# Two attention-time weight blocks: the join on VectorE cut in halves and the five steps after the load spread over half-steps

## The chip, the cores and the metric

The kernel runs on one core of one Trainium2 chip. The metric is the device time of one execution in microseconds (us); the kernel before took 747.65 us (median of 3 runs, 746.45 to 749.12). A core has five engines that each work through their own instructions in order: TensorE (PE, with its weight loads PEld), VectorE (DVE), ScalarE (ACT), GpSimd (POOL) and SyncE (SP, which issues most DMAs).

## The reference

Attention with a learned relative-position bias, for 4 batches of 8 heads, 576 positions, 64 channels, and then a feed-forward layer over all 2304 tokens:

```
scores = q @ k.T / sqrt(64) + bias          # bias: a small MLP of log-distances, 8 heads
attn   = exp(scores - max);  attn /= attn.sum() + 1e-9
x      = (attn @ v)  as [2304, 512]
h = x @ w_in                                 # 512 x 2048
g = h if h >= 1, 0 if h <= -1, else (h + 1)**2 / 4
out = g @ w_out                              # 2048 x 512
```

The feed-forward weights arrive as 64-bit integers' bytes (each element 8 bytes in memory) and are turned into 32-bit floats on the chip. Each float operand of a matmul is split into a high part (type fp32r) and a low remainder, and the products high x high, high x low, low x high are summed.

## The kernel before, in words

The program has three stages. First the bias is made (lines 217 to 350). Then the attention runs over 16 units `n` (line 624): a unit is two heads of one batch, with 5 row groups `k` each (128 rows for `k` 0 to 3, the last 64 rows of both heads together for `k` = 4). Last comes the feed-forward part over blocks of tokens.

In one attention unit, for every row group and both heads `j`: PE makes scores into a PSUM tile `S` (lines 455 and 456, two tiles in turn, so the next but one score waits until DVE has read this one); DVE adds the bias, writes `e` to SBUF and takes the row's extremum (line 458; line 478 for the tile `S_L` of `k` = 4); ACT takes the exponential (line 465); PE transposes `e` into PSUM tiles `T` (line 521; four in turn, shared with `O` and `R`). A transposed tile is split into `hi` and `lo`. For some tiles ACT casts `hi` (line 496) and DVE subtracts for `lo` (line 497). For `T_0_1`, `T_2_0`, `T_2_1`, `T_3_0` and `T_3_1` ACT copies the tile to SBUF as `c` (line 501), `hi` is cast by POOL (line 503, `T_0_1` and `T_3_0`) or by DVE (line 505, the other three), and POOL subtracts for `lo` (line 506). Then PE multiplies with the values (lines 559 and 561): `O_0` for the first half of the rows (`hi_0`, `lo_0`), `O_1` for the second half (`hi_1`, `lo_1`); within each, the five `hi` products stand ahead of the five `lo` products. After `O_1`, PE transposes the row sums into `R` (line 545), which closes a unit. Unit n's `O_1` and `R` stand on PE among the scores of unit n + 1: what the trace shows between two `R` is one unit's work, shifted. POOL also makes the low parts of keys (`ls`, line 136, two instructions) and values (`vs`, line 136), and issues the load `qa` (line 167); DVE casts `kh` (line 163) and `vs` (line 178).

Which instruction stands where on an engine is decided when the program is built: a scheduler orders them by its own cost estimates, except those marked with `keep` or `pool`, which stay in the order in which the code issues them (on their engine). So an edit at one place can move unmarked neighbours on every engine.

Into the attention's half-steps (`step`, line 621: `10 * n + i_`, ten to a unit) the kernel plans other work by the table `WQ`: four weight blocks, `(f, o)` = (0,0), (0,1), (1,0), (1,1), are loaded at half-steps 49, 59, 89, 99 and made from half-steps 53, 63, 93, 103 on, so in units 5, 6, 9 and 10. The making has five steps (`weight_ahead`, line 94): `shift` and `sign` on ACT (lines 105 and 112), `join` on DVE (line 116: an or of the shifted digits and the sign, 128x512, in place in the tile `a`), `high` on DVE (line 121: a cast of `a` to `w0h` or `w1h`) and `rest` on POOL (line 125: the remainder `w0l` or `w1l`). The other 28 blocks are made with the same function during the feed-forward part. The tiles `raw` and `a` are single buffers: the next load into them waits for their last reader.

Of the kernel before, what the change touches and what calls it, by code (L numbers as in the profile page):

```python
# [10 lines left out]
I32 = mybir.dt.int32  # L11
U16 = mybir.dt.uint16
AF = mybir.ActivationFunctionType
ALU = mybir.AluOpType
# [6 lines left out]
NT, DM, DFF = B * S, H * D, 2048  # L21
# [26 lines left out]
def attn_cpb_moe_kernel(ctx, tc, qk, vL, cb, win, wout, lw, ident, ii, out):  # L48
    nc = tc.nc
# [38 lines left out]
    def ring(o, i):  # L88
        return [rpool[i % 3].tile([P, DM], F32R, tag=f"w{o}{x}", name=f"w{o}{x}{i}") for x in "hl"]
# [4 lines left out]
    def weight_ahead(f, o, rp):  # L94

        w = {}
        src = wout[f * P : f * P + P] if o else win[f]

        def load():
            w["raw"] = rp.tile([P, DM, 2], I32, tag="raw", name=f"raw{f}{o}")  # L100
            nc.sync.dma_start(out=w["raw"].rearrange("p a b -> p (a b)"), in_=src.bitcast(I32))

        def shift():
            raw = w["raw"]
            keep(nc.scalar.activation(raw[:, :, 0], raw.bitcast(U16).rearrange("p a (b c) -> p a b c", c=2)[:, :, 0, 1], AF.Identity, scale=2.0**-13, bias=floor_s))

        def sign():
            if f < 2:
                w["a"] = rp.tile([P, DM], F32, tag="a", name=f"a{f}{o}")
            else:  # L110
                w["a"] = full[o, f]
            keep(nc.scalar.activation(w["a"], w["raw"][:, :, 1].bitcast(F32), AF.Prelu, scale=2.0**-112, alpha=-(2.0**32)))

        def join():
            t = w["a"].bitcast(I32)
            keep(nc.vector.scalar_tensor_tensor(out=t, in0=t, scalar=3, in1=w["raw"][:, :, 0], op0=ALU.logical_shift_left, op1=ALU.bitwise_or))

        def high():
            if f > 1:
                parts[o, f] = ring(o, f)  # L120
            keep(nc.vector.tensor_copy(parts[o, f][0], w["a"]))

        def rest():
            h, l = parts[o, f]
            keep(nc.gpsimd.tensor_tensor(out=l, in0=w["a"], in1=h.bitcast(F32), op=ALU.subtract))

        return load, shift, sign, join, high, rest

    qkv, bias = {}, {}
# [8 lines left out]
    def keep(ins):  # L138
        tc.keep_in_program_order(ins)
# [277 lines left out]
    with ExitStack() as ph:  # L417
# [173 lines left out]
        def plan(T, f):  # L591
            jobs.setdefault(T, []).append(f)
# [13 lines left out]
        for fo, (T, T1) in WQ.items():  # L606
            load, *fs = weight_ahead(*fo, rps[0])
            plan(T, load)
            for i, f in zip((0, 0, 1, 1, 2), fs):
                plan(T1 + i, f)  # L610

        def store_x(all_=False):
# [86 lines left out]
    with ExitStack() as ph:  # L699
# [197 lines left out]
        for f in range(2, NF):  # L897
            for o in range(2):
                m = 2 * f - 4 + 3 * o
                jobs[m] = weight_ahead(f, o, rps[m % 3 > 0])  # L900
# [12 lines left out]
        for k in range(2):  # L913
            t = T1 + 1 + 12 * k
# [17 lines left out]
        for blk in (0, TB):  # L932
            for m in range(2 * NF):
                f, j = m // 2, m % 2
# [4 lines left out]
                c = gp.tile([P, TH], F32, tag="c", name=f"c{blk}_{m}")  # L939
# [47 lines left out]
        for g in range(NG2):  # L987
            blk, f = b2, 2 * g
            for s_ in range(NS):
                t = NS * g + s_  # L990
# [110 lines left out]
```

## Time and profile before

| | us |
|---|---|
| median of the runs | 747.65 |
| profiled execution | 747.49 |
| its span, first to last instruction | 745.7 |
| units 5, 6, 9, 10, from `R` to `R` | 17.59, 17.35, 17.59, 17.31 |
| unit 3, which has neither a weight block nor another planned job | 15.96 |

The profiled execution is 1.8 us longer than its span, and 0.16 us under the median. In the rows below, times are us from the start of the span unless marked ns; a row of a timeline gives start, duration, engine, line, operation, output and inputs by name, shape, count, and in brackets how long the engine sat idle before it and what ended that.

### The profile page before, as it was taken

The numbers are of one execution on the slowest core, as the hardware profiler recorded it, in microseconds if no ns is written. First come the engines' busy times: TensorE is split into PE (matmuls) and PEld (weight loads), VectorE is DVE, ScalarE is ACT, GpSimd is POOL, SyncE is SP. The second block draws the span as 40 slices with busy tenths as digits, with TensorE's granted clock in tenths as the row PEclk, the third lists the DMA queues.
The fourth block names the chain that finished last, engine by engine and source line by source line (L and its number), as shares of the span: only waits on it lengthen the run. The fifth ranks groups of instructions, "written<-read, shape, count | busy, mean of one in ns | idle before, by whom it ended". The sixth has DMA issues, their size and how long they took to land. (4 is left out here: it accounts for less than half of the span.)

```text
span 745.7 us, 13716 instructions
## 1 busy us (share of the span) xinstructions
PE 701.6 (94%) x4640; PEld 620.3 (83%) x4640; DVE 541.5 (73%) x1047; ACT 516.4 (69%) x1151; POOL 519.2 (70%) x440
## 2 busy tenths in 40 slices
PE   5687999999999999999999999999999998999997
PEld 2234899998988889889988898898989987888896
DVE  7899888888898898886876866354465557666653
ACT  8896989888888889877565656444534446666563
POOL 8986777888878888852667677466655645666652
PEclk9999999999999999999999999999999999999999
DMA  8887799977997898634355554133021002000002
GB/s 231 239 268 227 200 250 244 305 204 183 263 234 196 201 256 205 156 113 147 113 177 162 189 155 138 43 96 75 1 65 32 1 4 82 1 1 1 0 1 85
DMA packets 58518, 103.37 MB, mean 139 GB/s; under 512 B 12480, under 2 KB 32464, under 8 KB 58448
## 3 DMA queue, kind: packets, MB, share of 16 engines
q1 hardware_dynamic: 56000, 92.44, 43.7%
q0 software_dynamic: 2304, 9.96, 6.4%
q8 instruction: 37, 0.61, 0.4%
q14 instruction: 33, 0.27, 0.1%
q10 hardware_dynamic: 144, 0.09, 0.1%
HBM read 67.38 MB, written 25.12 MB: 124 GB/s over the span
## 5 line engine op out<-in xcount | busy, mean ns | idle before, releaser
L951 POOL TENSOR_TENSOR gl<-c,gh 128x384 fp32r<-128x384 f32 x64 | 70.9, 1107 | 104.2 <-issue 86.8
L506 POOL TENSOR_TENSOR lo<-c,hi 128x512 fp32r<-128x512 f32 x75 | 101.5, 1369 | 29.7 <-DVE hi L505 27.1
L716 PE MATMUL y<-w1h,gl 128*128 128x512 f32 x288 | 114.0, 396 | 0.0
L716 PE MATMUL y<-w1l,gh 128*128 128x512 f32 x288 | 113.7, 395 | 0.0
L716 PE MATMUL y<-w1h,gh 128*128 128x512 f32 x288 | 112.0, 389 | 0.0
L465 ACT ACTIVATE e<-e,mx 128x576 f32<-128x576 f32 x128 | 100.6, 790 | 12.7 <-DVE mx L458 12.6
L458 DVE CUSTOM_DVE_ANT_0 e<-S,bias 128x576 f32<-128x576 f32 x128 | 94.3, 750 | 12.6 <-PE S L456 12.0
L455 PE MATMUL S<-kh,qa 128*128 128x288 f32 x256 | 78.4, 323 | 6.8 <-DVE mx L458 4.6
L769 ACT ACTIVATE c<-c,half_s 128x384 f32<-128x384 f32 x64 | 39.4, 616 | 60.7 <-DVE c L766 60.7
L456 PE MATMUL S<-ls,qa 128*128 128x288 f32 x256 | 72.3, 300 | 0.0
L521 PE MATMUL T<-id_s,e 128*128 128x128 f32 x512 | 70.7, 274 | 1.3 <-DVE lo L497 0.8
L977 POOL TENSOR_TENSOR gl<-c,gh 128x384 fp32r<-128x384 f32 x32 | 32.8, 1024 | 50.0 <-issue 23.3
L716 PEld LDWEIGHTS y<-w1h,gl 128*128 128x128 f32 x288 | 54.0, 187 | 11.6
L521 PEld LDWEIGHTS T<-id_s,e 128*128 128x128 f32 x512 | 58.7, 142 | 4.1 <-DVE lo L497 1.3
L284 ACT ACTIVATE u<-lw,nthr 128x576 f16<-128x576 f32 (+17 forms) x104 | 57.7, 644 | 5.1 <-PE B L303 2.7
L716 PEld LDWEIGHTS y<-w1l,gh 128*128 128x128 f32 x288 | 54.0, 187 | 8.0
L716 PEld LDWEIGHTS y<-w1h,gh 128*128 128x128 f32 x288 | 54.1, 188 | 7.7
L303 PEld LDWEIGHTS <-qh 128*32 128x32 f16 x704 | 19.1, 102 | 49.2 <-issue 21.2
L455 PEld LDWEIGHTS S<-kh,qa 128*128 128x128 f32 x256 | 48.2, 188 | 11.7 <-DVE mx L458 8.7
L772 DVE TENSOR_TENSOR c<-h,c 128x384 f32<-128x384 f32 x64 | 35.5, 554 | 26.8 <-ACT c L769 26.0
L286 POOL TENSOR_SCALAR u<-lw,thr 128x576 f16<-128x576 f32 (+17 forms) x36 | 51.5, 1442 | 4.3 <-PE B L303 3.1
L947 ACT CAST gh<-c 128x384 fp32r<-128x384 f32 x64 | 32.9, 513 | 30.7 <-DVE c L772 28.7
(264 smaller groups left out, 2117.5 us busy)
## 6 DMA issues: line engine op xcount, KB each, us to landing
bias_d<-y SPq DMA_DIRECT2D x36, 295.5 KB
qk<-in_qk_dram SPq DMA_DIRECT2D x16, 608.0 KB
qa<-in_qk_dram POOLq DMA_DIRECT2D x16, 608.0 KB, 7.0
x<-xT SPq DMA_DIRECT2D x48, 192.0 KB
raw<-in_win_dram SPq DMA_DIRECT2D x16, 512.0 KB
raw<-in_wout_dram SPq DMA_DIRECT2D x16, 512.0 KB
v<-in_vL_dram SPq DMA_DIRECT2D x16, 320.0 KB
qa<-ls SPq DMA_DIRECT2D x32, 152.0 KB
```

The lines of the kernel that those rows point to most:

```text
L284: tc.keep_in_program_order(nc.scalar.activation(u[:, :n_], lw1[:, :n_], AF.Sigmoid, bias=nthr[:, m : m + 1], scale=STEEP))
L286: EN[x].tensor_scalar(out=u[:, :n_], in0=lw1[:, :n_], scalar1=thr[:, m : m + 1], scalar2=None, op0=ALU.is_gt)
L455: nc.tensor.matmul(ps[:, hf, :HS], qs[:, qc], kh[:, kc : kc + HS], start=True, stop=False)
L456: nc.tensor.matmul(ps[:, hf, :HS], q0[:, qc], kl[:, kc : kc + HS], start=False, stop=True)
L458: nc.vector.tensor_tensor_reduce(out=ev.rearrange("p (a b) -> p a b", a=2), in0=ps[:, :, :HS], in1=bias[k][:, S * j : S * j + S].rearrange ...
L465: lambda ev=ev, j=j: nc.scalar.activation(ev, ev, AF.Exp, bias=mx[:, j : j + 1], scale=-1.0, accum_out=sm[:, 4 * j + k : 4 * j + k + 1])
L506: r = nc.gpsimd.tensor_tensor(out=lo, in0=m, in1=hi.bitcast(F32), op=ALU.subtract)
L521: nc.tensor.transpose(ps[:, tb, :], e[:, c0 : c0 + P], id_s)
L716: a = nc.tensor.matmul(out, w, x, start=start, stop=stop)
L769: keep(nc.scalar.activation(c, c, AF.Square, scale=0.5, bias=half_s))
L772: keep(nc.vector.tensor_tensor(out=c, in0=h, in1=c, op=ALU.max))
L951: keep(nc.gpsimd.tensor_tensor(out=gl, in0=c, in1=gh.bitcast(F32), op=ALU.subtract))
```

## The change

`join` takes a range of columns. For the first two `f` (the four blocks made in the attention) the function returns `first_half` and `second_half` in its place, so there are six steps after the load, and they are planned at half-steps T1 + 0, 0, 1, 2, 3, 4 (shift, sign, first half, second half, high, rest), where it was T1 + 0, 0, 1, 1, 2 (shift, sign, join, high, rest).

```diff
-        def join():
-            t = w["a"].bitcast(I32)
-            keep(nc.vector.scalar_tensor_tensor(out=t, in0=t, scalar=3, in1=w["raw"][:, :, 0], op0=ALU.logical_shift_left, op1=ALU.bitwise_or))
+        def join(c=slice(0, DM)):
+            t = w["a"].bitcast(I32)[:, c]
+            keep(nc.vector.scalar_tensor_tensor(out=t, in0=t, scalar=3, in1=w["raw"][:, c, 0], op0=ALU.logical_shift_left, op1=ALU.bitwise_or))
+
+        def first_half():
+            join(slice(0, DM // 2))
+
+        def second_half():
+            join(slice(DM // 2, DM))
...
+        if f < 2:
+            return load, shift, sign, first_half, second_half, high, rest
         return load, shift, sign, join, high, rest
...
             load, *fs = weight_ahead(*fo, rps[0])
             plan(T, load)
-            for i, f in zip((0, 0, 1, 1, 2), fs):
+            for i, f in zip((0, 0, 1, 2, 3, 4), fs):
                 plan(T1 + i, f)
```

What this does to the order on the engines is shown for unit 5 on two of them. In these rows the number behind a name is a buffer's, `lo_1` and `hi_1` are the parts of the second half of the rows, and `c` is ACT's copy of a transposed tile. Lines of the kernel after are 8 higher from line 134 on, and 6 higher for the cast and the remainder.

POOL before, from the remainder of the weight block on:

```order
L125 TENSOR_TENSOR w0l_120<-a_2863,w0h_119 128x512
L506 TENSOR_TENSOR lo_1_2921<-c_2927,hi_1_2920 128x4x128
L506 TENSOR_TENSOR lo_1_2921<-c_2936,hi_1_2920 128x4x128
L136 TENSOR_TENSOR vs_2954<-v_2769,vs_2954 128x10x64
L167 DMA qa_112<-in_qk_dram 64x2x1216
L503 CAST hi_1_2920<-c_3011 128x4x128
L506 TENSOR_TENSOR lo_1_2921<-c_3011,hi_1_2920 128x4x128
L506 TENSOR_TENSOR lo_1_2921<-c_3020,hi_1_2920 128x4x128
```

and now:

```order
L514 TENSOR_TENSOR lo_1_2921<-c_2927,hi_1_2920 128x4x128
L514 TENSOR_TENSOR lo_1_2921<-c_2936,hi_1_2920 128x4x128
L131 TENSOR_TENSOR w0l_120<-a_2863,w0h_119 128x512
L144 TENSOR_TENSOR vs_2955<-v_2769,vs_2955 128x10x64
L175 DMA qa_112<-in_qk_dram 64x2x1216
L511 CAST hi_1_2920<-c_3012 128x4x128
L514 TENSOR_TENSOR lo_1_2921<-c_3012,hi_1_2920 128x4x128
L514 TENSOR_TENSOR lo_1_2921<-c_3021,hi_1_2920 128x4x128
```

The remainder `w0l` has moved behind the first two `lo_1`; the rest of POOL's row stands as it did. Units 6, 9 and 10 show the same move.

DVE before, in the same unit, from the join on:

```order
L116 SCALAR_TENSOR_TENSOR a_2863<-a_2863,raw_2727 128x512
L458 ISA e_3_2906,mx_3_2905<-S_3_0_2907,bias_3_2400 128x576
L458 ISA mx_3_2905 128x1
L121 CAST w0h_119<-a_2863 128x512
L497 TENSOR_TENSOR lo_0_2815<-T_1_0_2884,hi_0_2814 128x4x128
L497 TENSOR_TENSOR lo_0_2815<-T_1_1_2891,hi_0_2814 128x4x128
L497 TENSOR_TENSOR lo_0_2815<-T_s_2898,hi_0_2814 128x256
L458 ISA e_3_2906,mx_3_2905<-S_3_1_2913,bias_3_2400 128x576
L458 ISA mx_3_2905 128x1
L505 CAST hi_1_2920<-T_2_0_2922 128x4x128
L505 CAST hi_1_2920<-T_2_1_2931 128x4x128
```

and now:

```order
L116 SCALAR_TENSOR_TENSOR a_2863<-a_2863,raw_2727 128x256
L466 ISA e_3_2906,mx_3_2905<-S_3_0_2907,bias_3_2400 128x576
L466 ISA e_3_2906,mx_3_2905<-S_3_1_2913,bias_3_2400 128x576
L466 ISA mx_3_2905 128x1
L505 TENSOR_TENSOR lo_0_2815<-T_1_0_2884,hi_0_2814 128x4x128
L505 TENSOR_TENSOR lo_0_2815<-T_1_1_2891,hi_0_2814 128x4x128
L505 TENSOR_TENSOR lo_0_2815<-T_s_2898,hi_0_2814 128x256
L116 SCALAR_TENSOR_TENSOR a_2863<-a_2863,raw_2727 128x256
L513 CAST hi_1_2920<-T_2_0_2922 128x4x128
L127 CAST w0h_119<-a_2863 128x512
L513 CAST hi_1_2920<-T_2_1_2931 128x4x128
```

The second half of the join stands after the three `lo_0`, the score `S_3_1` ahead of them, and the cast `w0h` between the two casts of `hi_1`. In units 6 and 10 the second half also stands behind the three `lo_0`, and the cast `w1h` stays ahead of both casts of `hi_1`.

## Rows read from the trace of the kernel before

**Rows 1.** Busy time of each engine, units 3, 5, 6 and 7, from `R` to `R`.

```profile
core 0: us, PE busy (x) PEld busy (x) DVE busy (x) ACT busy (x) POOL busy (x), PEclk, DMA share, GB/s
123.45:139.41 15.96, 15.88 (x126) 15.36 (x124) 14.25 (x33) 14.61 (x38) 13.39 (x12) 1.00 0.99 251
156.54:174.13 17.59, 16.43 (x126) 15.51 (x124) 16.02 (x35) 15.53 (x40) 14.27 (x13) 1.00 0.74 197
174.13:191.48 17.35, 16.63 (x126) 15.36 (x124) 15.39 (x33) 15.45 (x42) 14.70 (x13) 1.00 0.83 202
191.48:208.29 16.81, 15.81 (x124) 15.16 (x122) 13.99 (x30) 14.44 (x40) 14.65 (x12) 1.00 1.07 277
```

**Rows 2.** Who PE waited for, 92 to 276 us (sum, times, longest).

```profile
PE S L455 <- DMA kh<-kh: 1.2, 2, 1.0
PE T L521 <- DVE lo L497: 0.8, 2, 0.4
PE O L559 <- DVE lo L497: 0.6, 2, 0.3
```

**Rows 3.** Timeline of DVE in unit 5, and one join of the feed-forward part.

```profile
158.60 1.60 DVE L116 SCALAR_TENSOR_TENSOR a<-a,raw 128x512 int32<-128x512 int32 x1
...
160.79 0.42 DVE L121 CAST w0h<-a 128x512 fp32r<-128x512 f32 x1
...
163.33 1.28 DVE L505 CAST hi<-T 128x512 fp32r<-128x512 f32 x2
...
359.73 0.68 DVE L116 SCALAR_TENSOR_TENSOR w<-w,raw 128x512 int32<-128x512 int32 x1
```

**Rows 4.** Timeline of POOL in unit 5.

```profile
158.36 1.29 POOL L506 TENSOR_TENSOR lo<-c,hi 128x512 fp32r<-128x512 f32 x1
161.29 1.29 POOL L125 TENSOR_TENSOR w0l<-a,w0h 128x512 fp32r<-128x512 f32 x1 [1.64 <-DVE w0h L121]
164.09 2.56 POOL L506 TENSOR_TENSOR lo<-c,hi 128x512 fp32r<-128x512 f32 x2 [1.51 <-DVE hi L505]
166.59 2.13 POOL L136 TENSOR_TENSOR vs<-v,vs 128x640 fp32r<-128x640 f32 x1
...
170.01 2.55 POOL L506 TENSOR_TENSOR lo<-c,hi 128x512 fp32r<-128x512 f32 x2
```

**Rows 5.** Timeline of PE in unit 5: `S_L`, the low products of `O_1_0`, `R`.

```profile
160.92 0.41 PE L476 MATMUL S_L<-kh,qa 128*128 128x288 f32 x1 [1.16 <-DVE mx L458]
...
171.93 0.75 PE L559 MATMUL O<-lo,vs 128*128 128x320 f32 x4
...
174.13 0.27 PE L545 MATMUL R<-id_s,sum 128*9 128x128 f32 x1
```

**Rows 6.** Timeline of DVE in unit 6.

```profile
176.31 0.76 DVE L458 CUSTOM_DVE_ANT_0 e<-S,bias 128x576 f32<-128x576 f32 x1 [0.47 <-PE S L456]
176.99 1.23 DVE L116 SCALAR_TENSOR_TENSOR a<-a,raw 128x512 int32<-128x512 int32 x1
```

**Rows 7.** Timeline of POOL in unit 6.

```profile
176.38 1.29 POOL L506 TENSOR_TENSOR lo<-c,hi 128x512 fp32r<-128x512 f32 x1
...
181.44 2.55 POOL L506 TENSOR_TENSOR lo<-c,hi 128x512 fp32r<-128x512 f32 x2 [0.92 <-DVE hi L505]
183.94 2.11 POOL L136 TENSOR_TENSOR vs<-v,vs 128x640 fp32r<-128x640 f32 x1
...
187.33 2.56 POOL L506 TENSOR_TENSOR lo<-c,hi 128x512 fp32r<-128x512 f32 x2
```

**Rows 8.** Timeline of PE in units 6 and 7.

```profile
189.28 0.75 PE L559 MATMUL O<-lo,vs 128*128 128x320 f32 x4
...
199.43 0.38 PE L455 MATMUL S<-kh,qa 128*128 128x288 f32 x1 [0.98 <-DMA kh<-kh]
```

**Rows 9.** Timeline of SP's queue in units 6 and 7.

```profile
186.08 0.33 SPq L185 DMA_DIRECT2D v<-in_vL_dram  x1
...
191.93 0.60 SPq L200 DMA_DIRECT2D kh<-kh  x1
```

## The prediction

> **What bounds the kernel now.** I read first the busy times by unit [rows 1]. A unit that makes a weight block takes 17.59 or 17.35 us, unit 3, which has no planned work, 15.96; PE is busy 16.4 to 16.6 us in the former, DVE 15.4 to 16.0. No engine alone fills a weight unit, so its length is set by waits that run from engine to engine, and one has to find the loop. The list of PE's waits [rows 2] and PE's own timeline [rows 5] show the small part that PE sees: 1.16 us ahead of `S_L` in unit 5, because `S_3_0` is read late by DVE, which is busy with the join; 0.8 and 0.6 us in units 6 and 10 for DVE's `lo`; 0.98 us in unit 7 for the copy of `kh`. PE never waits for POOL's `lo` there. The timelines of POOL and DVE then show the loop. In unit 5 POOL idles 1.64 and 1.51 us [rows 4], both times for DVE, and `w0l` stands between the two waits. From 164.09 on, when DVE's cast of `T_2_0` releases it, POOL has no gap: two `lo_1`, `vs`, the load `qa`, a cast, two `lo_1`, then `ls`. The products of `O_1_0` with the low parts need the first of the later pair of `lo_1`, which ends half way through that pair, at 170.01 + 2.55 / 2 = 171.29; PE starts them at 171.93 [rows 4, 5]. So POOL is 0.64 us ahead of PE there. In unit 6 the same two times are 187.33 + 1.28 = 188.61 and 189.28: 0.67 us [rows 7, 8]. The feed-forward part has no changed instruction and only starts earlier or later.
>
> **The join in halves.** The join takes 1.60 us in unit 5 and 1.23 in unit 6, 0.68 in the feed-forward part where POOL is idle [rows 3, 6]. POOL's `lo` ends at 158.36 + 1.29 = 159.65, 1.05 us after the join's start, and in unit 6 at 177.67, 0.68 after it [rows 4, 7]: both times 0.55 us remain. So the join stands still while POOL's instruction runs and then takes 0.55. The first half starts at the same place, so it stands still for the same 1.05 us and then takes about 0.28: 1.33, and `S_3_0` is read 0.27 us earlier. If the half cost half of 1.60, this would be 0.80 us. I take 0.27 and keep 0.80 as the other end. The second half is 0.3 to 0.4 us (half of 0.55 to 0.68), as POOL is idle then. Together the halves cost 0.0 to 0.1 us more than the join, once in each of four units.
>
> [...]
>
> **The cast `w0h` and DVE's way to `T_2_0`.** In units 5 and 9 the cast (0.42 us [rows 3]) moves from ahead of DVE's cast of `T_2_0` to behind it. That cast, which starts POOL's gapless stretch, so comes about 0.42 - 0.1 = 0.3 us earlier. But `w0h` then begins as POOL's first `lo_1` is released. POOL started at 164.09, some 0.1 us after DVE's first cast had ended (163.33 + 1.28 / 2 = 163.97), so DVE starts first and POOL stands still for the other 0.3 us. I take the two as cancelling: POOL's stretch starts where it did. In units 6 and 10 the cast stays ahead and the start moves 0.1 us later by the halves.
>
> **The remainder `w0l`, `w1l` on POOL.** This decides. It costs 1.29 us [rows 4] and was hidden by POOL's wait for DVE; behind the first two `lo_1` nothing hides it, and it puts off `vs`, `qa` and the later `lo_1` by 1.29 us. What is late next are the low products of `O_1_0`: POOL was 0.64 us ahead of them, so PE gets them 1.29 - 0.64 = 0.65 us late, and behind them in PE's queue stand `O_1_1`, `R` and the next unit's scores. Whatever PE gains earlier in the unit is lost in this wait. Part of it may go another way: `vs` (128x640) took 2.13 us [rows 4], where 1.29 us for 128x512 would make 1.29 x 640 / 512 = 1.61; I put the other 0.52 down to DVE's cast of `kh`, which `w0l` now meets in its place. If all of that came off, 0.65 - 0.52 = 0.13 would be left. But the standstill only passes to the other instruction, so I keep 0.65. With 0.05 for what the halves add, unit 5 is **0.7 us longer**.
>
> Unit 6 starts 0.7 us late, and since DVE waits there for PE's score `S_3_0` (0.47 us, [rows 6]), its part up to the cast of `T_2_0` moves with PE. Then 0.1 for the halves + 1.29 for `w1l` - 0.67 that POOL was ahead: **0.7 us longer**, 1.4 for the pair of units.
>
> **The loads behind `vs`.** SP issues the load `v` at 186.08, when POOL has finished `vs` (183.94 + 2.11 = 186.05), since it writes the buffer that `vs` reads; the bias loads and then the copies of `kh` stand behind it [rows 7, 9]. PE waits 0.98 us for the first of these in unit 7 [rows 8]. `vs` now ends 0.7 + 0.1 + 1.29 = 2.1 us later, PE comes to the wait 1.4 us later, so the wait may grow by 0.7 us; or by nothing, if the transfers take up the slack. The DMA engines are full in that unit (share 1.07, [rows 1]), which speaks for transfers that are only moved; in unit 11, the other such place, the wait was 0.2 us (1.2 us for both [rows 2]), which leaves less behind it. Between these ends I take the middle, 0.35.
>
> **The sum.** Per pair of weight units 1.4 + 0.35 = 1.75 us, two pairs (5 and 6, 9 and 10): 3.5 us. The profiled execution takes 747.49 us, 0.16 less than the median shown; 747.49 + 3.5 = 751.0 us. The other edits cost nothing that I can find: `raw` is read to its end some 3 us later, but the next load into it has ten half-steps, a whole unit of over 15 us [rows 1], and the exponentials that ACT does in another order stay ahead of PE's need for the low parts.
>
> **Rivals.**
> *Faster.* POOL's delay doesn't reach PE, because `vs` shrinks by its 0.52 us and the 0.64 cover nearly all the rest. Then the waits count: 0.27 to 0.80 us ahead of `S_L` in units 5 and 9, and up to 0.6 us of the 0.7 in units 6 and 10 (1.4 for both, [rows 2]), since `w1h` and a part of the join no longer stand ahead of `lo`. That is 2 x (0.27 + 0.6) = 1.7 to 2 x (0.80 + 0.6) = 2.8 us: about 745.2. It decides as soon as `w0l` costs less than 0.64 us on POOL's way to `O_1`. Against it: POOL's stretch is gapless in both units.
> *No change.* The change does what I say on POOL, but the wait for `kh` takes it up: the transfers end when they did, PE loses its 1.4 us in waits that are there anyway (0.98 and 0.2 us), and 2.8 - 1.2 = 1.6 us remain: 749.1.
> *Slower still.* POOL's `lo_1` starts ahead of `w0h`, DVE stands still for 1.29 us, and the cast of `T_2_1` and the reading of `S_L` come some 0.9 us later in units 5 and 9, with the whole 0.7 us of the loads: 2 x (1.4 + 0.6 + 0.7) = 5.4 us, of the 0.9 only 0.6 counted as PE waits for POOL anyway: 752.9.
>
> [...]
>
> **Chances and range.** My forecast 0.50, slower still 0.15, no change 0.22, faster 0.13. About what a measurement of this kernel can tell from no change is 0.3%, 2.2 us. The slower cases lie beyond it (0.65), the no-change case within (0.22), the faster case half-way across, counted as faster for 0.11 and as no change for 0.02. The range leaves out most of the faster case and the far end of slower still: 746.8 to 753.2. The slower case alone has 749.9 to 752.9.
>
> **What would show it.** In the trace after: the first half of the join in unit 5 takes 1.2 to 1.4 us, not 0.8; POOL's `w0l` runs at about 166.6 with no idle time ahead of it; PE waits 0.5 to 0.8 us at `O_1_0`, for POOL's `lo`, in units 5, 6, 9 and 10, where it never waited; these units take about 18.2 us; the wait for `kh` in unit 7 is over 0.98 us. I am wrong if PE meets no wait for POOL there, or if units 5 and 6 together are no longer than 34.94 us.

## The result and the profile after

| | kernel before | changed kernel | ratio (95% interval) |
|---|---|---|---|
| first comparison, median of 5 runs each, us | 747.14 (745.73 to 749.12) | 754.65 (751.29 to 755.31) | 1.0071 (1.0046 to 1.0096) |
| second comparison, 28 and 11 runs, us | 748.21 (744.94 to 752.53) | 752.95 (749.58 to 757.38) | 1.0069 (1.0044 to 1.0093) |

The brackets behind the medians are the lowest and the highest run. The change makes the kernel 0.7% slower, some 5 us; the ratio is not that of the medians, which lie 7.5 us apart in the first comparison and 4.7 in the second. The forecast was 3.5 us slower (751.0 against 747.49), so the sign was right and the size too small; the first median lies above the range given, the second inside it.

Two executions of the changed kernel were profiled, both with a span of 749.4 us. In the first one unit 4, where nothing is changed, was 0.7 us longer, with idle time of PE ahead of a score whose copy of `kh` SP had issued 2.4 us later than in the second (141.81 and 139.45); in the second it was not. That the copy is the reason is read from these times only. The time from `R` to `R`, by unit:

| unit | before | after, first profile | after, second profile | second less before | forecast |
|---|---|---|---|---|---|
| 4 | 17.13 | 17.81 | 17.15 | 0.0 | 0 |
| 5 | 17.59 | 17.38 | 18.20 | +0.6 | +0.7 |
| 6 | 17.35 | 17.34 | 17.36 | 0.0 | +0.7 |
| 7 | 16.81 | 19.10 | 19.11 | **+2.3** | +0.35 |
| 8 | 17.51 | 17.20 | 17.22 | -0.3 | 0 |
| 9 | 17.59 | 18.16 | 18.16 | +0.6 | +0.7 |
| 10 | 17.31 | 17.36 | 17.34 | 0.0 | +0.7 |
| 11 | 16.06 | 16.51 | 16.37 | +0.3 | +0.35 |
| 12 | 17.02 | 17.60 | 17.74 | +0.7 | 0 |

So the sum is made up of other parts than the forecast's: units 6 and 10 lose nothing, unit 7 alone loses half of it all. First the view that answers to [rows 1], of the changed kernel's first profile: busy times of units 5, 6 and 7, with the granted clock behind POOL.

```profile
core 0: us, PE busy (x) PEld busy (x) DVE busy (x) ACT busy (x) POOL busy (x), PEclk, DMA share, GB/s
157.13:174.51 17.38, 17.05 (x127) 15.52 (x125) 15.43 (x36) 15.64 (x41) 13.04 (x12) 1.00 0.73 199
174.51:191.85 17.34, 16.81 (x126) 15.35 (x124) 14.25 (x34) 15.45 (x41) 14.78 (x13) 1.00 0.80 192
191.85:210.95 19.10, 17.29 (x125) 16.80 (x123) 13.43 (x30) 14.49 (x38) 15.46 (x14) 0.91 1.06 269
```

The waits of PE, which answer to [rows 2], from the first profile again:

```profile
PE S L463 <- DMA kh<-kh: 1.8, 1, 1.8
PE S_L L484 <- DVE mx L466: 1.1, 2, 0.9
PE O L567 <- POOL lo L514: 1.0, 3, 0.4
```

The wait ahead of `S_L` stood in the kernel before as

```profile
PE S_L L476 <- DVE mx L458: 2.3, 2, 1.2
```

and in the second profile, which unit 4 does not disturb, the last two lines are

```profile
PE S_L L484 <- DVE mx L466: 1.8, 2, 0.9
PE O L567 <- POOL lo L514: 1.2, 4, 0.4
```

Three things changed there. PE now waits for POOL's `lo`, which it never did. Its waits for DVE's `lo` (0.8 and 0.6 us before) are gone, and the two ahead of `S_L` are 0.27 us shorter each (in the first profile the one of unit 5 is only 0.20 us, behind the disturbed unit 4). And the wait for the copy of `kh`, 0.98 and 0.23 us before in units 7 and 11, is 1.8 us in unit 7; in unit 11 there are 0.4 to 0.5 us, which the profiles put down to DVE's cast of `kh`. The timeline of POOL in unit 5, answering to [rows 4], shows the remainder at its new place, without idle time ahead of it:

```profile
163.61 2.66 POOL L514 TENSOR_TENSOR lo<-c,hi 128x512 fp32r<-128x512 f32 x2 [4.18 <-DVE hi L513]
166.23 1.83 POOL L131 TENSOR_TENSOR w0l<-a,w0h 128x512 fp32r<-128x512 f32 x1
168.02 1.56 POOL L144 TENSOR_TENSOR vs<-v,vs 128x640 fp32r<-128x640 f32 x1
...
170.86 2.55 POOL L514 TENSOR_TENSOR lo<-c,hi 128x512 fp32r<-128x512 f32 x2
```

It takes 1.83 us there in the place of 1.29: it now meets DVE's cast of `kh` (165.74 to 166.92), and `vs` takes 1.56 in the place of 2.13. The second profile's DVE and POOL in unit 5, undisturbed, answer to [rows 3, 4]:

```profile
158.55 1.33 DVE L116 SCALAR_TENSOR_TENSOR a<-a,raw 128x256 int32<-128x256 int32 x1
...
163.63 0.41 DVE L127 CAST w0h<-a 128x512 fp32r<-128x512 f32 x1
...
163.78 2.66 POOL L514 TENSOR_TENSOR lo<-c,hi 128x512 fp32r<-128x512 f32 x2 [4.18 <-DVE hi L513]
```

The half of the join takes 1.33 us for half of the columns: the number forecast. Unit 7 is where the time is lost. Here is SP's queue ahead of it and PE's timeline in it, in the first profile, answering to [rows 8, 9].

```profile
185.44 1.11 SPq L399 DMA_DIRECT2D xr<-rT  x2
186.96 0.33 SPq L193 DMA_DIRECT2D v<-in_vL_dram  x1
187.38 0.38 SPq L440 DMA_DIRECT2D bias<-bias_d  x1
...
192.79 0.65 SPq L208 DMA_DIRECT2D kh<-kh  x1
```

```profile
200.54 0.37 PE L463 MATMUL S<-kh,qa 128*128 128x288 f32 x1 [1.81 <-DMA kh<-kh]
...
202.13 1.91 PE L529 MATMUL T<-id_s,e 128*128 128x128 f32 x8
...
206.16 1.05 PE L529 MATMUL T<-id_s,e 128*128 128x128 f32 x8
```

The load `v` is issued when POOL's `vs` ends (185.38 + 1.55 = 186.93), 0.9 us later than before, and the bias loads behind it on SP's queue move with it (187.38, was 186.51). The copy of `kh` is issued 0.9 us later too, but there SP stands longer for POOL's `ls`, which is as much later. PE waits 1.81 us. And then something that the prediction did not have: eight transposes take 1.91 us and, four microseconds later, eight of the same shape 1.05. The view of a single stretch says why.

```profile
201.40:204.80 3.40, 3.40 (x17) 3.38 (x16) 1.61 (x5) 1.25 (x3) 1.68 (x4) 0.50 0.93 317
```

From 201.4 to 204.8 TensorE's granted clock is 0.50, where it is 1.00 on the mean of units 5 and 6. Of the 2.3 us of unit 7, 1.81 - 0.98 = 0.83 are the wait; I put the other 1.45 down to this stretch. An experiment below (e4, the remainder behind `vs`) bears that out: there PE waits 1.66 us at the same place, the clock stays at 1.00, and the unit takes 17.39 us in the place of 19.10. The second profile shows the same as the first (a wait of 1.90 us, the eight transposes behind it 1.91 us, a mean clock of 0.91 in unit 7).

### The profile page after: what moved, and what is told of

Read it like the earlier page. It is cut to its first block, busy times and chain, and to the rows that moved or that the text cites. A ratio compares the mean times of both kernels' runs of the same rounds, so it can differ in the third digit from the quotient of the medians.

```text
span 749.4 us, 13711 instructions
## 1 busy us (share of the span) xinstructions
PE 705.0 (94%) x4640; PEld 622.1 (83%) x4640; DVE 537.9 (72%) x1051; ACT 517.0 (69%) x1151; POOL 518.8 (69%) x440
## 4 chain that ended last, share of the span: by engine, by line
PE 61%; DVE 10%; POOL 5%; DMA 5%; ACT 5%; issue 3%; SPq 2%; DVEq 0%; ACTq 0%; POOLq 0%
PE y L724 21%; PE h L724 13%; PE p L724 7%; PE O L567 6%; PE T L529 4%; PE S L463 3%; PE S L464 2%; POOL lo L514 2%; DMA bias<-bias_d 2%; DVE lo L505 2%; PE O L569 2%; DVE e L466 1%; DMA raw<-in_wout_dram 1%; PE S_L L484 1%; SPq L399 1%
## 5 line engine op out<-in xcount | busy, mean ns | idle before, releaser
L463 PEld LDWEIGHTS S<-kh,qa 128*128 128x128 f32 x256 | 48.8, 191 | 13.1 <-DVE mx L466 7.8
```

The costliest lines, as they stand in the source:

```text
L463: nc.tensor.matmul(ps[:, hf, :HS], qs[:, qc], kh[:, kc : kc + HS], start=True, stop=False)
```

## The experiments

The changed kernel was timed again beside the first three experiments; this is the second comparison above.

> The changed kernel once more, on the chip on which the three others of this group run. Theory 1 (the remainder, late on GpSimd, puts off the loads behind the values' low part and so PE's wait for the copy of kh in unit 7) and theory 2 (the halves and the cast, and the order that they give VectorE, TensorE and ScalarE) both expect what was measured: 0.5 to 1.0% slower than the kernel before, some 751 to 755 us; in its profile PE's wait for kh in unit 7 over 1.5 us.

**The remainder's place on POOL.** Three kernels differ in the half-step of the remainder; the digits are the half-steps of the table behind T1. The first (e1) has the join whole and DVE's order of before, and moves the remainder alone.

```diff
 # from the kernel before
-            for i, f in zip((0, 0, 1, 1, 2), fs):
+            for i, f in zip((0, 0, 1, 1, 4), fs):
```

> The kernel before with the remainder alone planned two half-steps later (0, 0, 1, 1, 4), join whole: GpSimd gets the order of the changed kernel, VectorE keeps that of before. Theory 1: most of the loss, 2.5 to 6 us slower than before, with PE waiting for GpSimd's low parts at O_1 and over 1.5 us for kh in unit 7. Theory 2: within 1 us of before.

Measured: 756.97 us, ratio 1.0110 (1.0074 to 1.0146). The move of the remainder alone costs more than the whole change, and more than the 6 us that theory 1 had at most. Unit 5 takes 18.34 us, unit 6 17.83, unit 7 22.39. PE waits in units 5, 6, 9 and 10 for POOL's `lo` (0.4 us each), and in unit 7 for `kh`:

```profile
205.52 0.58 PE L455 MATMUL S<-kh,qa 128*128 128x288 f32 x1 [4.46 <-DMA kh<-kh]
```

The second (e2) is the rest of the change, with the remainder put back ahead of the first two `lo_1`:

```diff
 # from the changed kernel
-            for i, f in zip((0, 0, 1, 2, 3, 4), fs):
+            for i, f in zip((0, 0, 1, 2, 3, 3), fs):
```

> The changed kernel with the remainder alone one half-step earlier (0, 0, 1, 2, 3, 3), so that it stands on GpSimd ahead of the first two low parts, as before the change; VectorE has the order of the changed kernel. Theory 1: the loss is gone, within 2 us of before or faster. Theory 2: 3 to 8 us slower than before, as the changed kernel.

Measured: 751.54 us, ratio 1.0025 (1.0002 to 1.0048). A part of the loss is gone, two thirds of it by the ratios (1.0025 for 1.0069) and a third by the medians (3.3 us over the kernel before, for 4.7); 3.3 us is more than the 2 us of theory 1 and lies within theory 2's range. The profiled execution shows why this run does not decide: the remainder has its old place, but not its old time. `w0l` now waits for the cast `w0h` behind DVE's first cast of `hi_1` and so holds the first `lo_1` and `vs` back. `v` is issued 4.90 us ahead of the `R` at which unit 7 starts, as in the changed kernel (4.89; before 5.40), and unit 7 takes 18.92 us, with a wait of 1.72 us for `kh` and the low clock behind it (the eight transposes at 203.59 take 1.91 us). Units 6 and 10 are 0.5 us shorter than before (16.83 and 16.81). In unit 4 a late copy of `kh` (a wait of 1.26 us) disturbs the comparison of unit 5.

The third (e3) has the remainder behind the later pair of `lo_1`:

```diff
 # from the changed kernel
-            for i, f in zip((0, 0, 1, 2, 3, 4), fs):
+            for i, f in zip((0, 0, 1, 2, 3, 8), fs):
```

> The changed kernel with the remainder later still (half-step T1 + 8): on GpSimd behind the later two low parts and ahead of the keys' low part ls. The values' low part and the load of v are no longer put off, but ls and so the issue of the copy of kh are, by some 1.3 us. Theory 1 as predicted (the loads queued behind v are what is late): PE's wait at O_1 gone, unit 7's wait for kh back to about 1 us, within 2 us of before. Theory 1b (it is the copy's own issue after ls that counts): wait in unit 7 over 1.5 us, 2 to 6 us slower. Theory 2: as the changed kernel, 3 to 8 us slower.

Measured: 748.87 us, ratio 1.0014 (0.9996 to 1.0031), which can't be told from no change. SP's queue in units 6 and 7:

```profile
186.40 0.33 SPq L193 DMA_DIRECT2D v<-in_vL_dram  x1
186.83 0.38 SPq L440 DMA_DIRECT2D bias<-bias_d  x1
...
193.48 0.60 SPq L208 DMA_DIRECT2D kh<-kh  x1
...
198.36 0.62 SPq L399 DMA_DIRECT2D xr<-rT  x1
```

The copy of `kh` is issued 0.7 us later than in the changed kernel's first profile and yet PE waits only 0.28 us for it in unit 7, which takes 16.14 us. So it is not its own issue alone that makes it late. What came back is lost elsewhere: unit 8 takes 19.78 us, with a wait of 1.97 us for a score behind DVE's `scale_x` and `vs`, and the low clock after it (0.91 on the mean of the unit). So the move of the remainder is enough for the whole loss (the first of the three), and at a still later place the same work costs nothing that the timing shows (the third). The halves and the moved cast by themselves are tried further down, and cost nothing either. By which way the place costs time, the next one was to tell.

**The load `v`, or something else behind POOL?** The remainder right behind `vs` (e4), so that `v` isn't put off but the later `lo_1` are:

```diff
 # from the kernel before
-            for i, f in zip((0, 0, 1, 1, 2), fs):
+            for i, f in zip((0, 0, 1, 1, 7), fs):
```

> The kernel before with the join whole and DVE's order untouched; only the remainder is planned at T1 + 7, so that on POOL w0l and w1l stand right behind vs, ahead of the load qa and of the later pair of lo_1. The load v is issued as early as in the kernel before, while the later lo_1 come 1.29 us later. Theory (the load v, put off behind vs, is what makes the wait for kh in unit 7 grow): the wait there stays at or under 1.0 us and TensorE keeps its full clock; only the low products of O_1_0 wait for POOL, 0.65 us in each of units 5, 6, 9 and 10, so ratio 1.002 to 1.004. Rival (anything 1.29 us later on POOL does the same, wherever it stands, because ls and so the copy of kh are late): the wait for kh is 1.7 us or more, unit 7 over 18.5 us, ratio 1.006 to 1.010.

Measured: 755.55 us, ratio 1.0101 (1.0066 to 1.0137). The theory in this form failed: the waits for `kh` are 1.66 us in unit 7 and 2.57 in unit 11 (behind this one the clock was low: the eight transposes at 276.00 take 1.91 us).

```profile
201.61 0.37 PE L455 MATMUL S<-kh,qa 128*128 128x288 f32 x1 [1.66 <-DMA kh<-kh]
```

The rival has the ratio, but its reason doesn't hold either: in the next kernel `ls` is late too, the copy of `kh` is issued 1.2 us later in the unit than before, and there is no such wait. SP's queue shows what both had overlooked:

```profile
187.06 0.33 SPq L185 DMA_DIRECT2D v<-in_vL_dram  x1
188.31 1.10 SPq L391 DMA_DIRECT2D xr<-rT  x2
189.50 0.54 SPq L432 DMA_DIRECT2D bias<-bias_d  x1
```

`v` goes as soon as `vs` has ended, but behind it stands `xr`: the reciprocal row sums for a block of the feed-forward input, loaded into a tile that the pool places in the single buffer `a`. So `xr` is the next tenant of `a`, and `w1l` is the last reader of the block in it. `w1l` runs from 187.00 to 188.28 on POOL, and `xr` is issued at 188.31. It is the same in the other kernels: before, `w1l` ends at 180.51 and the first `xr` follows at 180.55; in the changed kernel it is 185.41 and 185.44. SP's own waits say the same: in the changed kernel's first profile, from 175 to 200 us, SP waits 2.9 us for `w1l` and 0.3 us for `vs`. The bias loads stand behind both on SP and come after them in each of these rows.

The same place as in e3, behind the later `lo_1`, with the join whole (e5):

```diff
 # from the kernel before
-            for i, f in zip((0, 0, 1, 1, 2), fs):
+            for i, f in zip((0, 0, 1, 1, 8), fs):
```

> The kernel before with the join whole and DVE's order untouched; the remainder at T1 + 8, on POOL behind the later pair of lo_1, ahead of ls: the place that cost almost nothing with the halves. Theory (only the remainder's place on POOL costs, the halves and the moved cast give back what PE saw of them, some 0.4 to 0.9 us per pair of units): units 5 and 6 as long as before or up to 0.5 us shorter, the wait for kh no longer than 1.0 us, a wait of 1 to 2 us in unit 8 for the low keys; ratio 0.999 to 1.004, at or above the 1.0014 of the version with the halves. Rival (the halves and the moved cast cost time on DVE, which the place on POOL hid in that version): under that version, 0.996 to 0.999.

Measured: 749.50 us, ratio 1.0014 (0.9988 to 1.0040), the same as with the halves. Units 5 and 6 take 17.59 and 17.66 us, so the gain of up to 0.5 us that was thought possible is not there. `xr` stands behind the copies of `kh` (issued at 199.00), and there is no wait in unit 7, which takes 15.91 us.

Set side by side, the profiles in which PE waited for `kh` in unit 7 show a regularity, with two exceptions: the copy of `kh` is there 12.1 to 13.2 us behind the first bias load, while its own issue lies 5.5 to 7.8 us back. (The last five rows are of kernels that follow below.)

| kernel | first bias load, us | copy of `kh` issued | PE's first product with it | from bias load | from the copy's issue | PE waited |
|---|---|---|---|---|---|---|
| before | 186.51 | 191.93 | 199.43 | 12.9 | 7.5 | 0.98 |
| changed, first profile | 187.38 | 192.79 | 200.54 | 13.2 | 7.8 | 1.81 |
| changed, second profile | 187.58 | 194.34 | 200.80 | 13.2 | 6.5 | 1.90 |
| e2, remainder back | 188.95 | 194.34 | 202.02 | 13.1 | 7.7 | 1.72 |
| e3, behind `lo_1` | 186.83 | 193.48 | 198.93 | 12.1 | 5.5 | 0.28 |
| e4, behind `vs` | 189.50 | 195.50 | 201.61 | 12.1 | 6.1 | 1.66 |
| e1, remainder late | 189.85 | 195.24 | 205.52 | 15.7 | 10.3 | 4.46 |
| e6, halves together | 187.98 | 193.39 | 200.26 | 12.3 | 6.9 | 0.33 |
| e7, cast late, first profile | 186.51 | 191.93 | 199.61 | 13.1 | 7.7 | 1.33 |
| the same, second profile | 185.84 | 191.25 | 198.43 | 12.6 | 7.2 | 0.82 |
| e8, changed, `v` late | 187.74 | 193.85 | 200.70 | 13.0 | 6.9 | 0.90 |
| e11, cast late, `v` late | 184.77 | 191.36 | 198.84 | 14.1 | 7.5 | 0.44 |

The DMA engines are full from the bias loads on (share 1.15 from 188 to 190 in the kernel before, 0.46 from 186 to 188), so my reading is that the copy comes when what was issued ahead of it has gone through. Why it is 12.1 us in some and 13.2 in others is not shown, and e1 and e11 don't fit; what held the copy of e1 2.5 us longer wasn't found. One kernel can also differ by 0.5 us from one execution to the next, as the two profiles of e7 do.

**The load `v` out of the way.** If this is so, the wait can be taken away without touching POOL. The load that stands ahead of the bias loads is that of unit 9 (and 13), needed a unit later, and goes behind the copies (e8):

```diff
 # from the changed kernel, in load_v
                 if n == 2:
                     after.enter_context(tc.issue_after(narrow[0].ins))
+                if n in (9, 13):
+                    after.enter_context(tc.issue_after(copied[n - 1].ins))
```

> The changed kernel; only the loads v of units 9 and 13, which stand on SP's queue in units 7 and 11 ahead of the bias loads and wait there for POOL's vs, are issued behind the copies of kh. They are needed a unit later. POOL's order, with w1l behind the first lo_1, stays. Theory (the wait for kh grows because POOL's later vs holds SP's queue at the load v, and the bias loads and the copies of kh come behind it): the first bias load is issued at about 186.6 in the place of 187.38, right behind the loads xr, and kh, which came 12 to 13 us behind it in the kernels so far, lands 0.8 us earlier, and up to 1.3 us more since v's 320 KB are out of the way; the wait in unit 7 falls from 1.8 to under 1.0 us, TensorE's clock stays at its full level there, unit 7 takes 16 to 17.3 us. What stays is the wait for POOL's lo in units 5 and 9: ratio 0.999 to 1.004. Rival (the copy of kh is late because its own source, or ls ahead of it, is late on DVE or POOL): the wait stays at 1.5 us or more, unit 7 over 18 us, ratio 1.005 or above.

Measured: 750.38 us, ratio 1.0027 (1.0009 to 1.0044), where the changed kernel has 1.0069 (1.0044 to 1.0093). The two intervals touch, and they come from different comparisons. In unit 7 this one came as expected: the first bias load follows the last `xr`, and the wait is 0.90 us, at full clock.

```profile
186.53 1.11 SPq L401 DMA_DIRECT2D xr<-rT  x2
187.74 0.54 SPq L442 DMA_DIRECT2D bias<-bias_d  x1
...
193.85 0.60 SPq L210 DMA_DIRECT2D kh<-kh  x1
...
199.41 0.35 SPq L195 DMA_DIRECT2D v<-in_vL_dram  x1
```

```profile
200.70 0.37 PE L465 MATMUL S<-kh,qa 128*128 128x288 f32 x1 [0.90 <-DMA kh<-kh]
```

```profile
192.93:209.82 16.89, 15.94 (x125) 15.13 (x122) 13.13 (x30) 14.25 (x38) 15.33 (x14) 1.00 1.08 274
262.66:281.90 19.24, 17.37 (x125) 16.78 (x122) 13.38 (x31) 14.70 (x38) 15.64 (x14) 0.91 1.03 250
```

(Unit 7 started 0.9 us later in this execution than in the second profile of the changed kernel; 187.74 to 200.70 is 13.0 us again.) Unit 7 takes 16.89 us in the place of 19.11. The copy of `kh` is issued 0.92 us behind unit 7's first `R`, as in the changed kernel's first profile (0.94), but PE has it 7.77 us behind that `R` in the place of 8.69: so in this execution it is what stands ahead of the copy, and not its own issue or `ls`, that moved it. The edit takes `v` itself out of the way as well as out of its place on the queue; the two are not separated.

What stays are the 0.6 us of units 5 and 9. And in unit 11, where the edit does the same, this execution goes against the theory: the first bias load is issued 5.0 us ahead of `R`, earlier than in the changed kernel (4.45), and yet PE waits 1.67 us for `kh`, with the low clock behind it (0.91 on the mean of the unit), where the changed kernel had waits of 0.4 to 0.5 us. So the profiled execution as a whole (751.06 us) is hardly shorter than those of the changed kernel (751.29 and 751.21); the gain stands on the timing and on unit 7.

The same edit on the kernel before (e9):

> The kernel before with the same two loads v behind the copies of kh, and nothing else. Theory: the first bias load of unit 7 is issued up to 1.9 us earlier than at 186.51 (behind the second xr at 183.51 + 0.61), the wait of 0.98 us for kh in unit 7 goes to 0.3 us or less, the 0.23 us in unit 11 too; unit 7 takes about 16 us in the place of 16.82: ratio 0.997 to 1.000. Rival (the gain is only passed on to the next wait for DVE in unit 8, 1.5 us): 0.999 to 1.001.

Measured: 748.25 us, ratio 1.0003 (0.9986 to 1.0019). The theory's gain did not come; the ratio is the rival's. Unit 7 takes 15.90 us, 0.9 less than before, without a wait for `kh`. But unit 8 takes 20.91:

```profile
217.08 0.38 PE L457 MATMUL S<-kh,qa 128*128 128x288 f32 x1 [1.05 <-DMA kh<-kh]
...
218.52 0.44 PE L457 MATMUL S<-kh,qa 128*128 128x288 f32 x1 [0.67 <-DMA kh<-kh]
```

The next unit's copy is late in its turn (the rival had a wait for DVE there), and the clock is low behind it: the eight transposes at 219.48 take 1.91 us, and the mean clock of the unit is 0.92. The DMA engines are full here (share 1.02 in unit 7), so it looks as if the transfers were the bound, and a wait that is taken away came back at the next one.

**The rest of the change.** The cut of the join alone, with nothing moved (e6):

```diff
 # from the changed kernel
-            for i, f in zip((0, 0, 1, 2, 3, 4), fs):
+            for i, f in zip((0, 0, 1, 1, 1, 2), fs):
```

> The changed kernel with both halves, the cast and the remainder where the kernel before has join, cast and remainder: only the cut of the instruction is left. Theory (the cut costs next to nothing): the two halves together take what the join took, up to 0.1 us more, twice in a pair of units; ratio 0.999 to 1.001. Rival (two instructions on DVE stand still behind POOL's once each, or the second start costs): 0.3 us or more in each of four units, ratio 1.0015 or above.

Measured: 748.21 us, ratio 1.0001 (0.9981 to 1.0021): two halves in a row cost what the whole did. The cast alone a half-step later, with POOL's order of before (e7):

```diff
 # from the kernel before
-            for i, f in zip((0, 0, 1, 1, 2), fs):
+            for i, f in zip((0, 0, 1, 2, 2), fs):
```

> The kernel before with the join whole and only the cast (w0h, w1h) a half-step later, planned in the same half-step as the remainder: DVE does the three lo_0 ahead of the cast, and in unit 6 the join ahead of the score S_3_0; POOL's order is the one of before, with w0l ahead of the first two lo_1. Theory (the part of the change on DVE is a gain, and only the remainder's place loses): w0l comes 1.2 us later, inside POOL's two waits of 1.64 and 1.51 us in unit 5, PE's waits for DVE's lo in unit 6 (0.6 and 0.5 us) become shorter, unit 6 is 0.3 to 0.6 us shorter, the wait for kh within 0.3 us of 0.98: ratio 0.996 to 1.000. Rival (the early parts of DVE's order give nothing, since the loop is closed by the wait for kh): 0.999 to 1.001 with the wait for kh longer by what unit 6 gained. Second rival (POOL's first lo_1 are pushed back by w1l in unit 6, where POOL's idle time ahead of them is only 0.92 us): slower, 1.001 to 1.003.

Measured: 747.26 us, ratio 0.9991 (0.9963 to 1.0019); a second profiled execution of the same kernel took 748.16 us.

> The kernel before with only the cast a half-step later, once more, for a second profile of it: units 5 and 6 together 33.3 to 33.8 us (34.94 before); the wait for kh in unit 7 between 0.3 and 1.6 us.

The units that make a block do get shorter: units 5 and 6 take 17.32 and 16.63 us in the second of these profiles, where it was 17.59 and 17.35, since the three `lo_0` no longer stand behind the cast. Their sum, 33.95, is just above the range expected. (The first profile has 16.96 and 16.63, but its unit 4 was 0.4 us longer.) But unit 7 then waits 1.33 us (first profile) or 0.82 (second) for `kh`, units 8 and 12 in the second up to 1.8 us for DVE, and no gain is left that the timing shows. Both edits together (e11):

> The kernel before with two edits that each left the time where it was: the cast (w0h, w1h) a half-step later, and the loads v of units 9 and 13 issued behind the copies of kh. Theory (units 5, 6, 9 and 10 keep their gain of 0.5 to 1.3 us per pair, and the wait for kh in unit 7, 0.8 to 1.3 us with the cast alone, goes to 0.3 us or less): units 5 and 6 together 33.6 to 34.0 us, unit 7 about 16 us, ratio 0.995 to 0.998. Rival (what PE gains in these units it loses in the next wait for a transfer, in unit 8 or 12, by the wait itself or by the lower clock behind it): ratio 0.999 to 1.001, with a wait for kh of more than 1 us in unit 8 or 12.

Measured: 748.06 us, ratio 1.0001 (0.9972 to 1.0031). Units 5 and 6 take 33.97 us, unit 7 16.50, but unit 8 19.21, with a wait of 1.99 us for DVE. Again the ratio is the rival's, though the wait is for DVE and not for `kh`. None of these versions beats the kernel before.

## Why the prediction was right, and where not

**The first half** was sized exactly: 1.33 us forecast and measured, `S_3_0` read 0.26 us earlier in the unit (3.32 us behind `R` in the second profile, was 3.58), PE's wait ahead of `S_L` 0.9 us in the place of 1.16. POOL's `lo` runs from 158.32 to 159.60 in the second profile, and the half, from 158.55 on, ends 0.28 us behind it: half of the columns, but the whole of POOL's 1.05 us before them. Had the half cost half of the join's 1.60 us, it would have been 0.80.

**The cast `w0h`** starts ahead of POOL's `lo`, by 0.15 us (163.63 and 163.78 in the second profile), as the forecast had it. So the case "slower still" fell: DVE is not held, its next cast starts at 163.96. The two were taken to cancel, with POOL standing still for 0.3 us; in fact POOL's stretch starts 0.26 us earlier in the unit (7.29 us behind `R`, was 7.55), and its first pair takes only 0.10 longer (2.66 for 2.56), though the cast ran on for 0.26 us behind POOL's start. So POOL was not held for the rest of the cast here: the 0.3 us of standstill was the author's estimate, and the run shows 0.10 us in its place.

**The remainder on POOL** is the right cause, and in units 5 and 9 the right size: +0.6 us for the 0.7 forecast. The low products of `O_1_0` come 0.5 us later in the unit (15.90 us behind `R`, was 15.39), where 0.65 was worked out; PE's waits for POOL there are 0.23 us in units 5 and 9, 0.37 in 6 and 10, where 0.5 to 0.8 had been named as a sign. The cast of `kh` passed its standstill on, as supposed: `w0l` took 0.53 us more, `vs` 0.57 less.

**Unit 6 was wrong.** The step that failed is "its part up to the cast of `T_2_0` moves with PE", with 0.1 us added for the halves. Before, POOL's `lo` started at 176.38, 0.6 us ahead of the join, which stood still behind it and took 1.23 us [rows 6, 7]. Now DVE is first:

```profile
177.12 0.42 DVE L116 SCALAR_TENSOR_TENSOR a<-a,raw 128x256 int32<-128x256 int32 x1
177.46 1.28 DVE L505 TENSOR_TENSOR lo<-T,hi 128x512 fp32r<-128x512 f32 x2
...
177.21 1.49 POOL L514 TENSOR_TENSOR lo<-c,hi 128x512 fp32r<-128x512 f32 x1
...
181.09 2.54 POOL L514 TENSOR_TENSOR lo<-c,hi 128x512 fp32r<-128x512 f32 x2 [2.39 <-DVE hi L513]
...
189.54 0.85 PE L567 MATMUL O<-lo,vs 128*128 128x320 f32 x4 [0.37 <-POOL lo L514]
```

POOL's `lo` starts at 177.21 in this profile, 0.09 us behind the half, and is the one that is held (1.49 us in the place of 1.29). With the cast `w1h` behind them too, the `lo_0` come 1.1 us earlier in the unit (2.95 us behind `R`, was 4.01). So PE's waits for them, which [rows 2] list at 0.4 and 0.3 us, vanish, and POOL is released 0.7 us earlier (6.58, was 7.31). This pays for `w1l`: the low products of `O_1_0` stand 15.03 us behind `R`, where it was 15.15. PE does wait for POOL there, 0.37 us, but it gets there that much earlier. e1, which moves the remainder without the DVE part, shows the unit without this: 17.83 us, +0.5. The forecast wrote "Whatever PE gains earlier in the unit is lost in this wait" and let only PE gain by it; POOL gained as well.

**The loads behind `vs`** were the right place, and a growth of 0.7 the top of the bounds, of which it took half; it was 0.8 to 0.9 us in unit 7. The two terms of that 0.7 were both too large: `vs` ends 1.1 us later and not 2.1, PE comes to the wait 0.45 us later and not 1.4 (second profile). Their difference, 0.6 us, is nearly the forecast's because the error in unit 6 stands in both: POOL was released 0.7 us earlier there, and PE did not lose the 0.7 us; the other 0.3 us is that the copy came 13.2 us behind the first bias load and not 12.9. That the order on SP decides PE's wait in unit 7 is shown by e8, which leaves POOL as it is and has the wait back at 0.90; in unit 11 the same edit did not do it. Of the two things that hold SP's queue, the forecast named one, `v` behind `vs`; the other, `xr` behind `w1l`, it passed over. It looked up the next load into `raw`, which "has ten half-steps", but not the one into `a`, which `xr` takes 0.04 us after the remainder. In the changed kernel `xr` costs nothing by itself, as `v` is held longer (186.93 against 185.41), but in e4 it is `xr` that holds the bias loads. No run moves `xr` alone.

**What was left out** is the clock: the wait that grew by 0.8 us cost another 1.45 us or so. It is the largest term of the difference, and no view of the kernel before was read for it. That the sum of 3.5 us came near the 3.7 of the profiled spans is therefore in part luck: 1.4 us were forecast for units 6 and 10 and did not come, and 1.45 came in unit 7 that were not forecast. Unit 12's +0.7 wasn't forecast either. It lies in three instructions of DVE, `scale_x` and the cast of `vs`, which meet other instructions of POOL than before (3.8 us from 279.40 to 283.22 in the second profile, 3.1 from 275.93 to 279.03 before); that this is the cause was only read, not tried.

The difference of the medians, 4.7 and 7.5 us in the two comparisons, is larger than that of the profiled spans, 3.7. The profiled executions of the changed kernel, 751.2 and 751.3 us, are among its shorter ones (749.6 to 757.4), so the profiles do not show what the longer ones lose. The mean granted clock of the timed executions is 0.989 (median) for the changed kernel and 0.9905 for the one beside it; more time at the lower clock may be a part of it, but this was not separated.

## What to carry to other kernels

An instruction that is moved on one engine also moves the time at which its operands' buffers come free: look up the next tenant of every tile that it reads (here `xr`, issued 0.03 to 0.04 us behind the remainder), on which queue that load stands, and what is queued behind it, not only who needs its result. Where a load for the unit after next waits in an in-order queue for a buffer, give the loads that are needed sooner a place ahead of it. This brought the changed kernel from 1.0069 to 1.0027, but gained nothing on the kernel before, where the DMA engines were full (share 1.02 in unit 7 with the edit). And a wait on TensorE can cost more than its length: in unit 7 of the changed kernel it was 0.83 us longer, with 3.4 us at a clock of 0.50 behind it, and the unit 2.3 us longer.

## What the hardware showed that was not expected

PE is busy for 94% of the span of the kernel before, and single waits were followed by a stretch at a granted clock of 0.50. Between 80 and 345 us, the profile of the kernel before and the first of the changed kernel have five idle times of PE of 1.5 us or more:

| kernel | PE idle, us | PE starts again | granted clock 0.50 |
|---|---|---|---|
| before | 1.54 | 211.86 | no |
| before | 1.59 | 326.77 | 327.7 to 331.1 |
| changed | 1.81 | 200.54 | 201.4 to 204.8 |
| changed | 1.62 | 283.81 | no |
| changed | 1.59 | 330.74 | 331.1 to 334.5 |

Each stretch is 3.41 us long and begins 0.4 to 0.9 us after PE has started again. In e1, behind 4.46 us, the low clock begins ahead of that moment (0.55 on the mean from 204 to 206 us, with PE starting at 205.52), and the products take 0.44 us in the place of 0.29 until 211.0. Idle times of 2.13 us in e6 (to 213.29) and 1.72 in e10 (to 211.08) were not followed by it, for the eight transposes behind them take 1.03 us; one of 1.72 in e2 was (1.91 us). So the length of the idle time alone did not decide it; what did is not shown. One more stretch, that of e9 shown above, stands behind two waits of 1.05 and 0.67 us. What such a stretch costs is seen in the eight transposes: 1.91 us in the place of 1.05.
